# A retention recurrence with a feed-forward block: the first two batches worked by halves of the heads, with the first weights in between

## Chip, cores, metric

One core of one Trainium2 chip. The metric is device microseconds of one execution, median over runs, each listed with its mean granted TensorE clock. Times of single runs stand in one column, the span of the profile (first to last instruction) is 1.7 to 2.2 us shorter than the time. The later calls ran on chips 1, 11 and 12; the record does not name the chip of the first call. Kernels of one call ran on the same chip beside runs of the kernel before.

## The reference, cut to what matters

```python
B, H, S, D = 4, 8, 768, 64
for t in range(S):                                   # per batch and head
    state = gamma * state + outer(k[t], v[t])
    y[t] = (q[t] @ state) / sqrt(D)
x = y.transpose(0, 2, 1, 3).reshape(B * S, H * D)    # 3072 x 512
h = x @ w_in                                         # 512 x 2048
out = maximum(0.01 * h, h) @ w_out                   # 2048 x 512
```

The weights come in as 64-bit floats (as words) and are turned into 32-bit ones on the chip; the recurrence is worked in chunks of 128 tokens: scores, a mask, values, and a state handed from chunk to chunk.

## The kernel before: the parts that the change touches

The kernel starts with four batches of chunk 0, and with the first four pieces of the weights, which all have to be loaded. `score` is 16 small matmuls (64x64 tiles), `values` 8, a step of `direct` is 4 matmuls of 128x128 by 256 columns with weights (each fp32 matmul shows as two instructions in a trace). `keep_busy(n)` issues n matmuls on zeros into a bank that nobody reads: filler.

```python
load_qk(0, 0); load_v(0, 0); load_qk(0, 1); load_v(0, 1)   # 0.52 + 0.26 MB each
load_piece(0); load_piece(1)                                # weights, 0.52 MB each
load_qk(0, 2); load_v(0, 2); load_piece(2); load_piece(3, words)
...
keep_busy(7)
score(0, 0)
# tables and spread: the decays, three matmuls on 8 rows of the table
masked(0, 0)
...
score(0, 1); values(0, 0); masked(0, 1); decay_v(0, 1)
keep_busy(1)
next_powers()                       # ScalarE: exponents of a piece
taken(0, 0, x)                      # VectorE: tokens into x
values(0, 1)
next_mantissas(lambda: taken(0, 1, x))   # VectorE: mantissas of the piece
next_powers()
score(0, 2)
keep_busy(3)
steps = direct(0, 0, x, parts[0][1], 0)
next(steps)                         # first product with weights
next_mantissas()
...
next(steps); values(0, 2); ...; score(0, 3); ...
next(steps)
for b in range(B): first_state(b, sums0)      # sums for the states
values(0, 3)
run(steps, {})                                # last product step
taken(0, 3, x); first_states_taken(sums0); add_sums(0, last=False)
```

## Time and profile before

| | before |
|---|---|
| time, median of 6 runs of the first call | 666.90 us (666.56 to 667.01) |
| span of the profile | 664.9 us |
| TensorE in the chain that ended last | 99% |
| first real matmul, first product with weights | 4.63 us, 14.09 us |
| sums for the states end, reads of chunk 1, batch 1 begin | 23.54 us, 33.45 us |

The lines that carry this are in the prediction.

### The profile page before, as it was taken

To read this page: it belongs to the slowest core of one execution; us is meant where nothing else is said; L and a number is where in the kernel's file an instruction comes from. 1 tells how busy PE (TensorE), PEld (TensorE's weight loads), DVE (VectorE), ACT (ScalarE), POOL (GpSimd) and SP (SyncE) were. 2 spreads that over 40 slices of the span, in tenths; PEclk is the share of its full clock that TensorE was granted. 3 is DMA by queue.
4 is the path that set the end of the run, shared out by engine and by line. 5 is a ranking of instruction groups with operands and counts; after the bars stand their busy time and mean duration, and the time that the engine had idled before them with its cause. 6 is when DMAs were issued, how large, how long until landed. Compare 5 with 4: busy or idle time off the path is not lost.

```text
span 664.9 us, 10405 instructions
## 1 busy us (share of the span) xinstructions
PE 659.4 (99%) x4505; PEld 573.6 (86%) x4505; DVE 373.9 (56%) x570; ACT 175.8 (26%) x322; POOL 20.1 (3%) x22
## 2 busy tenths in 40 slices
PE   8999999999999999999999999999999999999998
PEld 5888888888888888888888888888888888888886
DVE  5789969889888676325543613663431444431342
ACT  5854555264261002212201311210221220221210
POOL 0000000000000111001000100100100000000000
PEclk9999999999999999999999999999999999999999
DMA  8920312313222453003012100301300001000001
GB/s 327 403 97 33 126 64 79 112 65 113 109 85 75 166 184 127 1 1 128 1 46 81 64 1 1 127 1 64 128 1 0 2 0 45 19 1 1 0 1 63
DMA packets 15758, 48.92 MB, mean 74 GB/s; under 512 B 1753, under 2 KB 2009, under 8 KB 15713
## 3 DMA queue, kind: packets, MB, share of 16 engines
q1 hardware_dynamic: 15696, 48.24, 20.1%
q8 instruction: 35, 0.57, 0.3%
q14 instruction: 11, 0.08, 0.0%
q10 hardware_dynamic: 16, 0.02, 0.0%
HBM read 41.97 MB, written 6.29 MB: 73 GB/s over the span
## 4 chain that ended last, share of the span: by engine, by line
PE 99%; DMA 1%; DVE 0%; issue 0%
PE B_o L414 13%; PE A_o L414 13%; PE C_o L414 12%; PE C_h L414 12%; PE B_h L414 12%; PE A_h L414 12%; PE D_o L414 6%; PE D_h L414 6%; PE ap L165 4%; PE yp L193 4%; PE d L436 2%; PE yp L184 2%; PE yp L208 1%; DMA qk<-in_qk_dram 1%; PE sums L208 0%; PE idle L626 0%
## 5 line engine op out<-in xcount | busy, mean ns | idle before, releaser
L414 PE MATMUL A_h<-x,w 128*128 128x256 f32 x368 | 87.0, 379 | 0.0
L414 PEld LDWEIGHTS A_h<-x,w 128*128 128x128 f32 x368 | 69.9, 190 | 9.6 <-issue 0.2
L414 PE MATMUL A_o<-g,w 128*128 128x256 f32 x288 | 68.0, 379 | 0.0
L449 ACT ACTIVATE g<-g 128x512 f32<-128x512 f32 x69 | 42.0, 630 | 92.4 <-DVE g L361 92.4
L414 PEld LDWEIGHTS A_o<-g,w 128*128 128x128 f32 x288 | 54.8, 190 | 7.4
L454 ACT COPY m<-A_h 128x512 f32<-128x512 f32 x23 | 13.4, 582 | 143.6 <-PE A_h L414 103.9
L361 DVE TENSOR_TENSOR m<-m,B_h 128x512 f32<-128x512 f32 x23 | 15.8, 686 | 55.5 <-PE B_h L414 55.5
L361 DVE TENSOR_TENSOR m<-m,B_o 128x512 f32<-128x512 f32 x16 | 11.0, 685 | 63.9 <-PE B_o L414 63.9
L238 DVE TENSOR_TENSOR x<-yp,dec 128x512 f32<-128x512 f32 x24 | 16.4, 689 | 49.7 <-PE yp L208 35.6
L414 PE MATMUL C_h<-t,w 128*128 128x256 f32 x184 | 44.1, 383 | 0.0
L414 PE MATMUL B_h<-x,w 128*128 128x256 f32 x184 | 44.1, 383 | 0.0
L414 PE MATMUL B_h<-t,w 128*128 128x256 f32 x184 | 43.5, 379 | 0.0
L414 PE MATMUL D_h<-t,w 128*128 128x256 f32 x184 | 43.5, 379 | 0.0
L414 PE MATMUL C_h<-x,w 128*128 128x256 f32 x184 | 43.5, 379 | 0.0
L414 PEld LDWEIGHTS C_h<-t,w 128*128 128x128 f32 x184 | 34.5, 190 | 5.5 <-issue 0.9
L414 PEld LDWEIGHTS B_h<-t,w 128*128 128x128 f32 x184 | 35.0, 190 | 4.7
L414 PEld LDWEIGHTS D_h<-t,w 128*128 128x128 f32 x184 | 35.0, 190 | 4.7
L414 PEld LDWEIGHTS C_h<-x,w 128*128 128x128 f32 x184 | 35.0, 190 | 4.7
L414 PEld LDWEIGHTS B_h<-x,w 128*128 128x128 f32 x184 | 34.5, 190 | 5.0 <-issue 0.3
L364 DVE TENSOR_TENSOR gd<-g,gd 128x512 f32<-128x512 f32 x48 | 37.1, 773 | 1.7
L170 DVE TENSOR_TENSOR am<-ap,mask 128x1024 f32<-128x1024 f32 x24 | 28.5, 1220 | 10.8 <-PE ap L165 10.8
L414 PE MATMUL B_o<-gd,w 128*128 128x256 f32 x144 | 34.0, 379 | 0.0
(118 smaller groups left out, 1019.0 us busy)
## 6 DMA issues: line engine op xcount, KB each, us to landing
raw<-in_weights_dram SPq DMA_DIRECT2D x31, 512.0 KB, 4.3
qk<-in_qk_dram SPq DMA_DIRECT2D x19, 512.0 KB, 3.8
kv<-in_kv_dram SPq DMA_DIRECT2D x17, 512.0 KB, 4.4
out_dram<-o SPq DMA_DIRECT2D x23, 256.0 KB, 2.1
in<-in_qk_dram SPq DMA_DIRECT2D x3, 512.0 KB, 8.7
in<-in_kv_dram SPq DMA_DIRECT2D x3, 512.0 KB, 8.5
kv<-in_kv_dram SPq DMA_DIRECT2D x4, 256.0 KB, 7.0
o_in<-in_qk_dram SPq DMA_DIRECT2D x2, 512.0 KB, 8.6
```

Of the source, the lines that this page charges most:

```text
L165: nc.tensor.matmul(ps[ts(u, 64), j, a, :], lhsT=x[ts(j, 64), 1, a, ts(u, 64)], rhs=x[ts(j, 64), 0, a, :])
L170: nc.vector.tensor_tensor(out=am.rearrange("p j a t -> p (j a) t"), in0=scores[c, b].rearrange("p j a t -> p (j a) t"), in1=mask.unsqueeze ...
L184: nc.tensor.matmul(ps[ts(i, 64), j, m, :], lhsT=st[b][ts(j, 64), a, :], rhs=x[ts(j, 64), 0, a, :], start=(m == 0), stop=False, skip_group_ ...
L193: nc.tensor.matmul(ps[ts(i, 64), j, m, :], lhsT=y[:, 1, 2 * a + j, :], rhs=am[:, j, a, :], start=(c == 0 and m == 0), stop=True, skip_grou ...
L208: nc.tensor.matmul(sp[ts(j, 64), a, :], lhsT=y[:, 0, 2 * a + j, :], rhs=y[:, 1, 2 * a + j, :], start=start, stop=True, skip_group_check=True)
L238: nc.vector.tensor_tensor(out=blocks, in0=ps[:, :, 0 : HP // 2, :], in1=gq, op=ALU.mult)
L361: nc.vector.tensor_tensor(out=out, in0=a, in1=b, op=ALU.add)
L364: nc.vector.tensor_tensor(out=out, in0=a, in1=b, op=ALU.subtract)
L414: nc.tensor.matmul(half, lhsT=block(w, sa)[:, k, ts(i, 128)], rhs=rhs[:, k, :], start=(first and (i == 0 or split) and n == 0 and k == 0), ...
L436: nc.tensor.matmul(banks[r][:, i, :], lhsT=block(2 * u, r + 2 * kh)[:, k, ts(i, 128)], rhs=x[:, 2 * kh + th, k, :], start=(step == 0 and i ...
L449: nc.scalar.activation(g[:, i], g[:, i], AF.Prelu, alpha=0.01)
L454: nc.scalar.copy(out=got["m1"], in_=ps)
```

## The change

Intent: let TensorE begin products with weights sooner. Only half of the first two batches is loaded ahead of the first two pieces of the weights; that half is scored, masked and multiplied, then comes the first product step, then the second half, and so on. For that, q, k and v of four heads lie next to each other in one array of 8 KB rows. All filler but the one at the start goes. The diff, cut to its core:

```diff
-    rows = t[0:H, 1:3].rearrange(...)[:, 0 : decay.shape[1]]
-    nc.scalar.dma_start(out=rows, in_=decay)
-    load_qk(0, 0)
-    load_v(0, 0)
-    load_qk(0, 1)
-    load_v(0, 1)
+    rows = t[:, 1:3].rearrange(...)[:, 0 : decay.shape[1]]
+    nc.gpsimd.memset(rows, 0.0)
+    nc.scalar.dma_start(out=rows[0:H], in_=decay)
+    nothing = t[:, 0, 0, 0:64].bitcast(BF16)
+    nc.vector.memset(t[:, 0, 0, 0:64], 0.0)
+    load_half(0, 0, 0)            # 3 KB of every 8 KB row: 0.39 MB
+    load_half(0, 1, 0)
     load_piece(0)
     load_piece(1)
+    load_half(0, 0, 1)
+    load_half(0, 1, 1)
 ...
-    keep_busy(7)
-    score(0, 0)
+    keep_busy(8)
+    score(0, 0, 0)                # first half of the heads
     # tables
+    score(0, 1, 0)
     # spread
+    first_values(0, (0,)); first_values(1, (0,))
+    begin_mantissas()
+    first_tokens_taken(0, x, (0,)); first_tokens_taken(1, x, (0,))
+    end_mantissas()
+    score(0, 0, 1)                # second half
     steps = direct(0, 0, x, parts[0][1], 0)
     next(steps)                   # k, kh swapped: the first half is enough for it
+    ...; score(0, 1, 1); next(steps); ...
+    first_values(0, (1,)); first_values(1, (1,)); ...; score(0, 2); next(steps); ...
 ...
     score(0, 3)
-    next(steps)
+    run(steps, {})                # last product step
+    first_values(3)
     sums0 = two_banks("sums0")
     for b in range(B):
         first_state(b, sums0)
-    values(0, 3)
-    run(steps, {})
```

## The prediction

> **What bounds the kernel now.** I read the page first, then the chain that ended last (whole span, then the first 45 us), then the order of instructions in time for the first 45 us, then the transfers.
>
> ```profile
> span 664.9 us, 10405 instructions
> PE 659.4 (99%) x4505; PEld 573.6 (86%) x4505; DVE 373.9 (56%) x570; ACT 175.8 (26%) x322; POOL 20.1 (3%) x22
> PE 99%; DMA 1%; DVE 0%; issue 0%
> ```
>
> TensorE is the bound: the chain is TensorE from its first real matmul to the end, and after 45 us it waits for nobody by more than 0.3 us. So only the start can pay, and a microsecond won there reaches the end only if nothing takes it back. The chain of the start, by start and length, says where the dead time is:
>
> ```profile
> 0.80 3.78 DMA qk<-in_qk_dram
> 4.63 1.75 PE ap L165 x32
> 7.88 1.03 PE ap L165 x32
> 8.91 1.02 PE yp L193 x16
> 9.94 0.32 PE idle L626
> 11.48 0.70 DVE x L238
> 12.23 1.10 PE ap L165 x32
> 13.34 0.75 PE idle L626 x3
> 14.09 3.45 PE d L436 x16
> 19.60 1.92 PE d L436 x8
> 21.53 2.02 PE sums L208 x64
> 23.54 0.88 PE yp L193 x16
> 24.42 3.65 PE d L436 x16
> ```
>
> The reader is to see that from 4.63 to 14.09 us TensorE does filler twice (0.32 and 0.75; these matmuls write a bank nobody reads) and stands for VectorE once (0.70); with small gaps that is about 2.0 us that serve nothing. From 14.09 on the chain has no gap. All that the change can win is a part of these 2.0 us.
>
> The filler is there because of the transfers:
>
> ```profile
> 9.55 0.69 ACT L334 ACTIVATE w<-raw 128x512 f32<-128x512 uint16 x1 [1.05 <-DMA raw<-in_weights_dram]
> 4.00:4.50 0.50, 0.50 (x2) 0.00 (x0) 0.00 (x0) 0.00 (x0) 0.00 (x0) 1.00 0.40 115
> 7.00:7.50 0.50, 0.50 (x2) 0.05 (x1) 0.50 (x1) 0.00 (x0) 0.00 (x0) 1.00 1.10 430
> ```
>
> ScalarE begins to unpack the first piece of the weights when it lands, at 9.55. In the table of stretches (last column GB/s) the transfers run at 410 to 430 once going, but between 4 and 6 us only at 115 to 300. From issue plus time to landing of each single load I get landing against the bytes queued up to it: 0.52 MB at 4.6 us, 0.79 at 5.5, 1.31 at 7.6, 1.57 at 8.3, 2.10 at 9.6, 2.62 at 10.9, 3.15 at 12.1, 3.93 at 14.0, 4.46 at 15.4, 5.24 at 17.3.
>
> **What the Trainium skill says.** "TensorE: Matmul & The Clock Gate", Part 1 (the HAM clock gate), says that the array runs at half rate until it has been busy for about 4 us. The trace agrees: the first score's matmuls take 417 to 471 ns until 5.9 us, then 269, which is why it takes 1.75 us against 1.03 later. The same page, section "HAM oscillation", says an idle stretch of some 3.4 us brings the half rate back; no run here shows that yet, and it matters, as the change takes all filler but the first out. "DMA: Bandwidth & Descriptors", the anatomy of one DMA, gives about 2 us fixed plus bytes at 436 GB/s, fitted on the GpSimd path. Here the first 512 KB took 3.78 us, against 3.2 by that fit, and the steady rate was 410 to 430; I use the landings of this trace.
>
> **The change, part by part.**
>
> Transfers. Before: qk0, v0, qk1, v1 (1.57 MB) stood ahead of the first piece of weights. After: two half-batches of 0.39 MB each (q, k and v of four heads) stand ahead. By the landings above: first half-batch near 4.1, second 5.5, weights piece 0 (1.31 MB) 7.6 instead of 9.55, piece 1 (1.84 MB) 8.9, the second halves (2.23 and 2.62 MB) 9.9 and 10.9, piece 2 12.1, piece 3 13.4, batches 2 and 3 at 15.4 and 17.3, as before. The bytes are the same.
>
> Warm-up. The zeroed tile is 64 columns instead of 256 and comes first on VectorE, so the filler begins near 1.1 instead of 1.40; eight at 0.427 end near 4.5. Score work begins at 4.5 instead of 4.63.
>
> TensorE to the first product with weights. Half score, cold: 0.85, to 5.4. Tables 0.31 + 0.22, to 5.9. Half score of batch 1: two scores in a row took 1.91 and one 1.03, so a half is 1.03 - 0.44 = 0.59, to 6.5. Spread 0.96, to 7.45. The two half values lie side by side, 1.02, to 8.5. Then the next half score waits for its data, 9.9 (1.4 dead), and ends at 10.5. The first product needs piece 0: landed 7.6, ScalarE 0.69, a copy 0.59 put between, 0.63 + 0.63, with hops 10.25, then VectorE 0.69: 10.95 (0.45 dead). VectorE's own work before that (two masks of 0.69, a decay near 0.4, 0.42 + 0.69 of the piece, two half takes of 0.42) fits in between.
>
> TensorE from there. One product step by itself is 1.92 (the row at 19.60), while two in a row are 3.45: now each step stands alone between small matmuls. 10.95 + 1.92 (step 0) + 0.59 + 1.92 (step 1; piece 1 ready at 12.9, in time) + 1.02 (both half values) + 1.03 (score 2), then a wait of 0.15 for piece 2, + 1.92 + 1.0 + 1.03 + 1.92 + 0.95 + 2.02 (the sums for the state) = 26.4; the first step of the second token half ends at 28.35. Before, that step ended at 28.07. So the same work is done 0.3 us later: 1.0 us of filler and the 0.7 of waiting are gone, but 1.4 + 0.45 + 0.15 of new waits and some 0.7 of smaller groups (0.47 for split product steps, 0.12 for each split score) take their place.
>
> After that. TensorE's order is the same, but VectorE's start of the next chunk moved: the sums used to end at 23.54, ahead of the last values, now they come last, at 26.4. Behind them stand on VectorE the states 1.22, the weight sums 2.14, then 4.23 from the mask of chunk 1, batch 0, to the end of the mask of batch 1 (in the trace 29.17 to 33.40): 26.45 + 1.25 + 2.1 + 4.23 = 34.05. The matmuls that read the state of batch 1 reuse the bank which that mask frees, and began at 33.52, 0.12 after it. They now begin near 34.15, 0.65 later. From 45 us on I expect no change: the loads of the later chunks become one of 1 MB instead of two of 512 KB, but GpSimd is idle for some 50 us between them. The hand sum is +0.65, or 667.5.
>
> **The rivals.**
>
> First rival: the weights come sooner than my landings say. The slow stretch of the transfers from 4 to 6 us may belong to what is issued then and not to the time. Piece 0 is the third transfer instead of the fifth; at 0.41 MB per us from the second half's 5.5 it lands at 6.8. The first product then starts at 10.2 to 10.5 (score of the second half at 9.2 to 9.9) and everything after is 0.5 to 0.7 earlier: 666.9, or less if the half groups cost less than 0.59. For it: the steady 430 GB/s directly after. Against it: the same number of transfers is issued by the same queue in the same first 3 us.
>
> Second rival: the change does what it was made for, the dead time falls from 2.0 to under 1.0, and nothing is handed back later: 665.5 to 666. It needs the landings of the first rival, cheap switching between tile sizes, and the sums to end before 25.6. Against it: the product cannot start earlier than about 3.3 us after piece 0 has landed (ScalarE's four steps and VectorE's one), whatever TensorE does.
>
> Third rival: without filler inside, TensorE's clock falls to half for a while. The dead stretches that I find are 1.4 and 0.45 us, under the 3.4 us of the skill; a fall would cost about 2 us and give 669. I hold it for unlikely.
>
> **Range and chances.** The hand sum gives +0.65; the first rival, about as likely, gives 0; the second gives -1. I set the point at 666.9, so no change within what I can tell, and the range 665.5 to 668.1, which holds all but the clock rival. Two per cent is 13 us, and all the dead time there is makes 2: 0.99 within 2%, 0.005 on either side.
>
> **What would show it right or wrong.** Piece 0's first step on ScalarE near 7.6 (rival one: 6.8); the first product near 10.95 (10.3) instead of 14.09; TensorE idle before the second half score, released by its load; the first step of the second token half ending near 28.35; the reads of chunk 1, batch 1, released by VectorE's mask near 34.15, with a TensorE wait of some 0.3 us that was not there; no filler after 4.5 us and no matmul slowed to 417 ns after 6 us. A wait that I did not find, before 45 us, or one in the later chunks where the 1 MB loads land, would make it wrong; so would a first product that comes later than 11.5.

## More of the kernel before

The order of instructions in time: the columns are start, length, engine, line, operation, tiles, shapes, count, and in brackets the idle time of that engine before it and what ended it. First the table of decays, which waits for nothing, then the reads of the state of chunk 1, batch 1 (as weight loads, PEld), which just wait for VectorE's mask:

```profile
6.31 0.38 PE L638 MATMUL tables<-t 8*128 8x8 f32 x2
...
33.45 0.43 PEld L184 LDWEIGHTS yp<-in,states 64*64 64x64 f32 x16 [0.17 <-DVE am L170]
```

## The result, and the profile after

| | before | after |
|---|---|---|
| median of 6 runs, us | 666.90 | 669.41 |
| all runs, us | 666.56 to 667.01 | 668.09, 668.24, 669.33, 669.50, 669.94, 670.38 |
| clock of these runs | (profiled run: 1.000) | 1.000, 1.000, 0.997, 0.997, 1.000, 0.995 |
| span of the profiled run (666.64 and 668.24 us) | 664.9 | 666.2 |

The ratio is 1.0036, with an interval of 1.0023 to 1.0049. Such ratios are the mean time of one kernel's runs over that of the other's of the same rounds, so not quite the ratio of the medians. The change made the kernel slower by 2.5 us in the median: "within 2%" held, the range (665.5 to 668.1) did not.

Two things are mixed in these 2.5 us. The two runs with the lowest times are 1.2 to 1.3 us above the kernel before; the other four lie 1.1 to 2.3 us above those two. I take the first part from the profile, which fell on a low run.

The page of the kernel after, its first lines and the chain's shares:

```profile
span 666.2 us, 10350 instructions
PE 659.4 (99%) x4502; PEld 572.4 (86%) x4502; DVE 372.1 (56%) x573; ACT 175.6 (26%) x323; POOL 22.2 (3%) x25
PE 97%; DVE 1%; DMA 1%; ACT 1%; issue 0%; POOL 0%; POOLq 0%
```

TensorE is as long at work as before (659.4), but now 3% of the chain is other engines. TensorE in order of time:

```profile
5.21 0.79 PE L182 MATMUL ap<-in 64*64 64x128 f32 x16 [0.57 <-DMA in<-in_heads_dram]
7.10 0.36 PE L703 MATMUL tables<-t 128*128 128x8 f32 x2 [1.09 <-DMA t<-decay_dram]
...
8.21 1.13 PE L711 MATMUL spread<-t 128*128 128x512 f32 x2
...
11.93 1.99 PE L494 MATMUL d<-x,w 128*128 128x256 f32 x8 [0.76 <-DVE w L415]
```

The first product with weights does come sooner, at 11.93 instead of 14.09. But the first half score starts later than the full one did (5.21 against 4.63), and TensorE waits 1.09 us for the table of decays, which nobody waited for before. The chain names that load, and what follows the sums:

```profile
1.58 5.39 DMA t<-decay_dram
...
25.59 1.89 PE sums L254 x64
...
27.50 1.23 DVE states L269
...
33.69 1.23 DVE am L191
...
34.96 0.67 PE yp L208 x16
```

The sums now end at 27.5 instead of 23.54, VectorE's states wait for them, and the reads of chunk 1, batch 1, begin at 34.96, 1.5 us later than before. From there the two kernels run nearly in step; the spans differ by 1.3, so some 0.2 comes back later.

### The profile page after: what moved, and what is told of

Same layout as the page of the kernel before. It is cut to its first block, busy times and chain, and to the rows that moved or that the text cites. A ratio compares the mean times of both kernels' runs of the same rounds, so it can differ in the third digit from the quotient of the medians.

```text
span 666.2 us, 10350 instructions
## 1 busy us (share of the span) xinstructions
PE 659.4 (99%) x4502; PEld 572.4 (86%) x4502; DVE 372.1 (56%) x573; ACT 175.6 (26%) x323; POOL 22.2 (3%) x25
## 4 chain that ended last, share of the span: by engine, by line
PE 97%; DVE 1%; DMA 1%; ACT 1%; issue 0%; POOL 0%; POOLq 0%
PE B_o L472 12%; PE A_o L472 12%; PE C_o L472 12%; PE C_h L472 12%; PE B_h L472 12%; PE A_h L472 12%; PE D_o L472 6%; PE D_h L472 6%; PE ap L182 3%; PE yp L215 3%; PE d L494 2%; PE yp L208 2%; PE yp L254 1%; DMA t<-decay_dram 1%; PE yp L226 0%; PE sums L254 0%
## 5 line engine op out<-in xcount | busy, mean ns | idle before, releaser
L283 DVE TENSOR_TENSOR x<-yp,dec 128x512 f32<-128x512 f32 x20 | 13.7, 688 | 47.4 <-PE yp L254 35.2
L422 DVE TENSOR_TENSOR gd<-g,gd 128x512 f32<-128x512 f32 x48 | 35.4, 737 | 1.7
L158 POOL TENSOR_TENSOR in<-in,dec 128x512 f32<-128x512 f32 (+1 forms) x19 | 20.9, 1102 | 459.3 <-DMA in<-in_heads_dram 260.5
```

The source lines that it names most:

```text
L158: engine.tensor_tensor(out=v[:, a:z], in0=v[:, a:z], in1=g[:, a:z].unsqueeze(3).to_broadcast([128, z - a, H // 2, D]), op=ALU.mult)
L283: nc.vector.tensor_tensor(out=blocks, in0=ps[:, :, 0 : HP // 2, :], in1=gq, op=ALU.mult)
L422: nc.vector.tensor_tensor(out=out, in0=a, in1=b, op=ALU.subtract)
```

## The experiments

All kernels gave correct results. I call a run disturbed when it is over 1.0 us above the fastest run of its own kernel (the kernel before and the changed kernel: of all their runs), and clean otherwise. The line is a rough one: two runs of e4 with a clock of 0.997 fall below it, and two of e6 lie just on it. "Cold" means at half rate: the matmuls take about twice as long as the same ones later. The counts are gathered here, and used below.

| run | what it is | runs | fastest, us | median, us | disturbed |
|---|---|---|---|---|---|
| before, all calls | 7 filler matmuls at the start | 40 | 666.42 | 666.90 (first call); 666.92; 667.84; 666.91 (chips 1, 11, 12) | 11 |
| changed, both calls | 8 at the start | 11 | 668.09 | 669.41; 670.18 | 8 |
| e1_decay | changed, decays early | 6 | 667.49 | 668.69 | 3 |
| e2_filler | changed, filler in the later waits | 6 | 668.10 | 669.55 | 3 |
| e3_sums | changed, sums ahead | 6 | 667.53 | 669.45 | 5 |
| e4_two | e1 and e3 | 6 | 666.71 | 668.16 | 3 |
| e5_full | e2 with 10 at the start | 6 | 668.09 | 668.26 | 0 |
| e6_best | e4 with 10 and later filler | 6 | 667.28 | 667.79 | 1 |
| e7_contig | changed, halves in one piece | 4 | 667.63 | 668.45 | 2 |
| e8_bare | before, no later filler | 6 | 666.53 | 666.73 | 2 |
| e10_warm | before, 10 at the start | 5 | 667.00 | 667.16 | 0 |
| e11_all | e6 with e7 | 5 | 667.65 | 667.86 | 0 |
| e12_lean | e4 with e7, 8 at the start | 6 | 666.97 | 669.10 | 5 |
| e13_nine | before, 9 at the start | 6 | 666.49 | 666.91 | 0 |
| e14_ten | changed, 10 at the start | 6 | 667.97 | 668.18 | 1 |
| e15_four | before, 4 at the start | 6 | 669.34 | 669.72 | 6 (counted from the fastest run of the kernel before, 2.9 us or more over it) |

The kernel before had 0 of 6 disturbed runs in the first call, and 2 of 11, 7 of 12 and 2 of 11 on chips 1, 11 and 12. (On chip 11, two calls share most of these runs.)

### The theory and its rivals

T: the load of the decays comes late and holds the tables, and with them the first product. H: the sums at the end of the chunk hand a loss back through VectorE. C: the spread of the runs is the array clock. Against T stands that ScalarE's chain behind the first weights sets the first product anyway; against H, that VectorE's wait only falls into a loss that TensorE has already; against C, that the transfers scatter.

### e1_decay

```diff
-    rows = t[:, 1:3].rearrange(...)[:, 0 : decay.shape[1]]
-    nc.gpsimd.memset(rows, 0.0)
-    nc.scalar.dma_start(out=rows[0:H], in_=decay)
+    rows = t[0:H, 1:3].rearrange(...)[:, 0 : decay.shape[1]]
+    nc.scalar.dma_start(out=rows, in_=decay)
```

> The changed kernel with the decay table on 8 rows again and its load issued at once, as before (no zero fill of 128 rows on GpSimd ahead of it). Theory T (the small load of the decays, issued at 1.58 us behind four big ones, lands at 6.96 and holds the tables, the decayed values and the first product): the load lands near 3 to 5 us, the tables run right after the first half score (near 6.0 instead of 7.10), the first product with weights moves from 11.93 to about 11.0, and the profiled run gets 0.6 to 1.0 us shorter than the changed kernel's best (668.1), so 667.1 to 667.5. Rival R1 (ScalarE's chain after the first piece of weights sets the first product anyway): the tables come early, but the first product stays at 11.7 to 11.9 and the time at 668. Theory C (the spread of the runs, 668.1 to 670.4, is the array clock that comes to full rate late or falls back, because TensorE waits between 4.6 and 12 us): here one wait of 1.1 us goes away, so fewer runs lie over 1 us above the fastest.

TensorE in order of time, run e1:

```profile
6.17 0.38 PE L702 MATMUL tables<-t 8*128 8x8 f32 x2
...
11.08 1.99 PE L494 MATMUL d<-x,w 128*128 128x256 f32 x8 [0.48 <-DVE w L415]
```

The wait ahead of the tables is gone, the first product comes 0.85 sooner, and the fastest run is 0.60 under the changed kernel's. T holds. The rival R1 does not: in both profiles ScalarE's copy of the spread, which hangs on the tables, starts 0.02 us after the spread ends (at 9.37, in e1 at 8.46), when its first step on the weights is already done, and the first product follows from there.

How a load of 24 KB can take 5.4 us is seen in the packets of its queue, counted by half microsecond: issued at 0.80 (kernel before and e1), its 16 packets move between 1.5 and 2.5 us; issued at 1.58, after the zero fill, none moves before 5.0, and the last after 6.5. In those 0.8 us the first two half-batches have been issued.

In e1 the first piece of weights also landed sooner (ScalarE began on it at 7.55 instead of 8.12). That is no accident of one run: with the halves read from wide rows, ScalarE began at 7.29 to 7.61 in the three profiles with the early issue (e1, e4, e6) and at 7.92 to 8.65 in the six with the late one; why, no run shows. It bears on the gain: at 8.12 + 0.68 the copy could not have begun before 8.80, so some 0.35 of the 0.85 us needed the sooner weights too.

On the spread of the times nothing can be concluded: three of six runs were disturbed, against four of six of the changed kernel's first call.

### e2_filler

```diff
     score(0, 0, 0)
+    keep_busy(2)
     # tables
-    score(0, 0, 1)
+    score(0, 0, 1)        # after 2 filler matmuls into its own bank
-    steps = direct(0, 0, x, parts[0][1], 0)
+    steps = direct(...)   # after 1 filler matmul into its own bank
```

> The changed kernel with filler matmuls put into its three waits (2 ahead of the tables, 2 ahead of the second half score, 1 ahead of the first product), nothing else. Theory C: the runs come together: all at 668.0 to 668.6 with a clock of 1.000, where the changed kernel has 668.1 to 670.4 with three clocks of 0.995 to 0.997. Rival (the spread comes from the transfers or the waits themselves, not from the clock): the spread stays near 2 us, median 669.4. The fastest run should not be faster than the changed kernel's fastest by more than 0.2 under either, since the filler takes away no wait.

Half right. No run had a clock under 1.000 any more (the changed kernel had four of eleven, so six runs do not prove it), but the runs fell into two groups: 668.10, 668.13, 668.39 and 670.70, 670.84, 670.92. So there are two kinds of disturbance: one that shows as a lower mean clock, and one of 2.5 us that the clock's record does not show.

### e3_sums and e4_two

```diff
     score(0, 3)
     ...
-    run(steps, {})
-    first_values(3)
     sums0 = two_banks("sums0")
     for b in range(B):
         first_state(b, sums0)
     load(1, 3)
+    first_values(3)
     decay_v(1, 0, nc.scalar)
+    run(steps, {})
```

> The changed kernel with the sums for the states ahead of the last values, and the last product step behind both, as before the change; the start is left alone. Theory H (part of the loss is handed back after the start: the sums come last, VectorE begins the states and the weight sums later and holds the reads of chunk 1, batch 1, until 34.96): the fastest run gets 0.5 to 1.0 us shorter (667.1 to 667.6), the reads of batch 1 no longer wait for VectorE's mask or by less than 0.2, the spread of the runs stays. Rival R2 (TensorE's own work has moved by the whole 1.3 us and VectorE's wait only falls into it): the time stays at 668.1 for the fastest.

> Both mends together: decay load first on 8 rows, and the sums ahead of the last values. If T and H are both right and add up: fastest run 1.3 to 1.9 us under the changed kernel's, 666.2 to 666.8, so level with or just under the kernel before (666.9). If they are one and the same slack: no better than the better of the two single ones. Theory C expects the spread of single runs to remain where TensorE still waits for loads between 8 and 11 us.

The fastest run of e3 is 0.56 under the changed kernel's, that of e4 1.38 under it (the sum of the two alone is 1.16). So H holds too, and the two add up. The profiles of both fell on disturbed runs, so the clean times are the evidence (e3 has only one clean run); the clean profile of e6 below, which has both mends, shows that the wait for VectorE is back to 0.17. Part of the gain of e3 is on TensorE: the last product step and the next one are neighbours again, 3.65 us for both instead of two of 1.92. With both mends the kernel is level with the kernel before (666.71 against 666.42 for the fastest run on that chip), not under it.

The profile of e4 fell on a run with clock 0.997, and shows what that is. The table of stretches; columns are the stretch, its length, busy time of TensorE, weight loads, VectorE, ScalarE and GpSimd with counts, granted TensorE clock, share and rate of the transfers:

```profile
7.00:8.00 1.00, 1.00 (x4) 0.24 (x4) 1.00 (x3) 0.39 (x1) 0.53 (x1) 1.00 1.01 414
...
8.50:9.00 0.50, 0.50 (x8) 0.50 (x6) 0.31 (x1) 0.50 (x2) 0.00 (x0) 0.50 1.10 442
9.00:10.00 1.00, 0.86 (x9) 0.48 (x7) 0.53 (x2) 0.97 (x3) 0.06 (x1) 0.50 1.02 411
...
12.00:13.00 1.00, 1.00 (x7) 0.81 (x5) 0.90 (x2) 0.81 (x2) 0.00 (x0) 1.00 1.06 432
```

The granted clock falls to 0.50 soon after 8.0 us and is back before 12. And yet TensorE was busy from 5.2 to 8 without a hole; before that it had one of 0.56 us, at 4.64.

The profile of e3 was cold in the other way: the spread took 2.07 us and the values after it 1.98 instead of 1.13 and 1.09, until about 13 us, with the clock recorded as 1.000. So half rate from the very start goes unrecorded, and the mean clock names only runs in which the clock falls after it had been full.

### e5_full, e6_best, e7_contig, e8_bare

e5 is e2 with `keep_busy(10)` at the start. e6 has the edits of e1 and e3, `keep_busy(10)`, and the later filler of e2 without the two ahead of the tables.

> The changed kernel with 10 filler matmuls at the start instead of 8 (to 5.3 us, so that the wait of 0.57 us ahead of the first half score is filled too) and the filler in the three later waits. The run with filler in the later waits alone had no clock under 1.000 any more, but still two groups of runs: three at 668.1 to 668.4 and three at 670.7 to 670.9. Theory C1 (the second group are runs in which the array did not come to full rate at 5 to 6 us, because the first filler ends before the first real work and leaves a hole): all six runs at 668.1 to 668.7. Rival (the late warm-up comes from where the clock's window happens to lie at the start, hole or no hole): still one to three of six runs near 670.8.

> All mends together: decays on 8 rows and loaded at once, sums ahead of the last values, 10 filler matmuls at the start, 2 ahead of the second half score and 1 ahead of the first product. If T, H and C1 are right: all six runs at 666.5 to 667.0, so level with the kernel before (666.9) with a spread under 0.6 us; the change then has no gain left to give even when every loss that I found is mended. If the late warm-up is luck alone: 666.6 for the fast ones and 669 for one to three of six.

On a chip where the kernel before had 7 of 11 disturbed runs in the same call, e5 had none of 6 (668.09 to 668.55), as expected under C1. The reason that C1 gives is not shown: in e5's profile the first half score is still cold, to about 6.5 us, with no hole ahead of it. In e6 three runs were at 667.3, two at 668.3 and one at 668.75 with clock 0.997, so none lay 2 us or more above the others, but the fastest was 667.28, not 666.5 to 667.0: ten filler matmuls end at 5.4 us and hold the first half score back. Its profile, a clean one:

```profile
5.43 0.67 PE L184 MATMUL ap<-in 64*64 64x128 f32 x16
...
10.87 1.99 PE L498 MATMUL d<-x,w 128*128 128x256 f32 x8
...
33.51 0.42 PEld L210 LDWEIGHTS yp<-in,states 64*64 64x64 f32 x16 [0.17 <-DVE am L193]
```

The first product is 3.2 us sooner than before the change and the reads of batch 1 are where they were (33.51 against 33.45). So where do the 3.2 us go? The chains of the two profiles answer it. Most of it was never a gain: a half score (0.60), two groups of half values (1.02) and a score (1.03) that used to stand ahead of the first product now stand behind it, 2.65 us of work that is moved and not saved. The rest goes to product steps that stand alone (0.46 for the first two, 0.07 for the third) and to a wait of 0.10. Together that is 3.28 us, and the sums begin at 21.59 instead of 21.53.

```diff
 # e7: an array of its own for the first two batches
-        fetch(c, b, m * HALF, (m + 1) * HALF)
+        nc.sync.dma_start(out=heads[c, b][:, m * HALF : (m + 1) * HALF], in_=first_in[m, b])
```

> The changed kernel with the first two batches' halves read from an own array in which each half-batch of 393 KB lies in one piece, instead of 3 KB of every 8 KB row; nothing else. In the changed kernel the first half-batch lands 4.4 us after its issue (at 5.2), though 0.52 MB of q and k before landed after 3.8, and the transfers ran at 150 to 220 GB/s from 2.5 to 4.5 us where they ran at 330 to 385 before. Theory L (it is the layout: pieces of wide rows are read slower while the transfers start): the first half-batch lands after 3.3 to 3.8 us, the rate between 2.5 and 4 us is over 300, and the first product starts up to 0.6 earlier. Rival (it is the start of the queue, whatever is read): landing again near 4.4 and the same rates.

The stretch from 2.5 to 4 us, in the kernel before, the changed kernel and e7 (the last column is GB/s):

```profile
2.50:4.00 1.50, 1.50 (x5) 0.45 (x3) 0.00 (x0) 0.19 (x1) 0.00 (x0) 1.00 0.91 362
```

```profile
2.50:4.00 1.50, 1.50 (x5) 0.46 (x3) 0.00 (x0) 1.00 (x1) 0.00 (x0) 1.00 0.88 164
```

```profile
2.50:4.00 1.50, 1.50 (x5) 0.45 (x3) 0.00 (x0) 1.00 (x1) 0.00 (x0) 1.00 1.04 342
```

The engines are as busy, but they move 164 GB/s where the source is a 3 KB piece of an 8 KB row, and 342 where it is in one piece. The first half score starts at 4.58 instead of 5.21. (The profile fell on a disturbed run, so its first product, at 12.93, says nothing.) Theory L holds for the start (later, past 6 us, the wide rows run at 416 as well). The fastest run is 0.46 under the changed kernel's.

```diff
 # e8, from the kernel before
-    keep_busy(1)
     next_powers()
 ...
     score(0, 2)
-    keep_busy(3)
```

> The kernel before with its four later filler matmuls taken out (1 after the first values, 3 ahead of the first product); the seven at the start stay. Question: is the fall of the clock in the changed kernel due to the filler that it took out? If yes: here too several of six runs show a clock of 0.995 to 0.997 and lie 0.8 to 2.5 us over the fastest, which is at 665.8 to 666.6 (up to 1.1 us of filler gone from the chain, though part of it only covered waiting for a load). Rival (what matters are the holes between 4.6 and 7.1 us, which this kernel hasn't): all runs within 0.7 us and clock 0.999 to 1.000.

Two of six disturbed (one at clock 0.994), about as in the kernel before (7 of 11 in this call); the fastest, 666.53, is 0.3 under its. So, as far as six runs tell, taking the later filler out is not what disturbs the runs. The profile fell on a run with the clock never raised at the start. The order of instructions, then two stretches:

```profile
7.34 2.05 PE L644 MATMUL spread<-t 8*128 8x512 f32 x2
...
11.23 3.04 PE L193 MATMUL yp<-am,kv 128*64 128x128 f32 x26
```

```profile
6.00:8.00 2.00, 2.00 (x17) 1.48 (x10) 1.30 (x2) 0.00 (x0) 0.00 (x0) 1.00 0.96 350
...
12.00:14.00 2.00, 2.00 (x22) 2.00 (x20) 1.27 (x3) 1.94 (x5) 0.00 (x0) 1.00 1.02 411
```

TensorE is busy without a hole from 1.40 us on, and the spread at 7.34 and the values at 11.23 still run at half rate. Holes cannot be the reason here. What TensorE does between 4.6 and 14 us are matmuls on 64x64 tiles, on 8 rows or into 64 columns; only the filler and the products with weights fill the array. That this is why it stays cold is a guess: no run here changed the tiles alone.

### e9_after, e10_warm, e11_all, e12_lean

e9 is the changed kernel unchanged. e10 is the kernel before with the change's small zeroed tile and `keep_busy(10)`. e11 is e6 with the edit of e7. e12 has the edits of e1, e3 and e7 and `keep_busy(8)`.

> The changed kernel as it is, beside the kernel before on this chip. On the last chip the kernel before itself had 7 of 11 runs at 667.8 to 670.2, on the first none of 6; so part of the difference on record may be luck of the clock. Theory A: the clean runs (clock full from 6 us on) of the two differ by 1.2 to 1.4 us (668.1 against 666.8), and disturbed runs (over 0.6 us above the cleanest of their kernel) are about as frequent in both on one chip, so that the median's 2.5 us is 1.3 of the kernel and the rest of the clock. Theory B: the change itself makes disturbed runs more frequent: at least four of six here against at most a third of the kernel before's runs of the same call.

Of five runs four were disturbed (669.69 to 670.57), against 2 of 11 of the kernel before beside them; the clean one is 668.19. Theory B holds: the changed kernel is disturbed more often. Its profile shows the spread at half rate (the clean profile has 1.13 and 1.09):

```profile
9.05 2.08 PE L711 MATMUL spread<-t 128*128 128x512 f32 x2
11.06 1.68 PE L226 MATMUL yp<-am,in 128*64 128x128 f32 x16
```

> The kernel before with ten filler matmuls at the start instead of seven, begun at 1.05 us like the changed kernel's (64 zeroed columns), else as it was. With ten at the start none of 12 runs of two kernels on the last chip stayed cold until 13 us, while the kernel before did in 3 of 11. Theory W (the late warm-up depends on how long the dense filler at the start lasts, since the small matmuls after it do not bring the clock up: in one profile TensorE was busy from 1.4 us without a hole and still cold at 13): no run of six above 669, clean runs 667.0 to 667.6, because the filler now ends at 5.4 instead of 4.5 and part of the 0.8 us is taken up by the later filler's place. Rival (chance of the chip): as many runs above 669.5 as the kernel before has in this call.

All five at 667.00 to 667.46, as expected, though the kernel before had only two disturbed runs in this call, both with a lower clock.

> All mends (decays early on 8 rows, sums ahead of the last values, ten filler matmuls at the start, three later) and the first halves read from an array of their own in one piece. In the run with that array alone the first half-batch landed by 4.6 instead of 5.2 and the first piece of weights 0.4 earlier. If the first product hangs on the first piece of weights (landing near 7.2, then 3.3 us): first product at 10.4 to 10.6 instead of 10.87, clean runs 666.7 to 667.0, none above 668.5. Rival: the transfers of the first 7 us move the same bytes, so the weights land at 7.5 as before and nothing is won: 667.3.

> Decays early on 8 rows, sums ahead of the last values, first halves in one piece; filler as in the changed kernel (eight at the start, none later). Clean runs: without the array of its own 666.7; with it the start is 0.3 to 0.5 earlier if the loads land earlier, so 666.2 to 666.5, under the kernel before's clean runs (666.4 to 667.1). Disturbed runs by the clock: two or three of six, up to 3 us above, as with eight filler matmuls before.

Both missed in their times: e11's fastest is 667.65 and e12's only clean run 666.97. In e11 the first product came at 11.62 instead of 10.4 to 10.6, in e12 the first piece of weights landed at 8.20 and the second half at 10.6. From e12, ScalarE's first step on the weights (from the chain: start, length, what), then the second half score (from the order of instructions):

```profile
8.22 0.67 ACT m_x L395
```

```profile
10.62 0.67 PE L183 MATMUL ap<-in 64*64 64x128 f32 x16 [2.02 <-DMA in<-in_first_dram]
```

What is gained at the start of the transfers is lost between 4 and 6 us (206 GB/s in e12 against 286 in e1). Why, I have not found out. In e12 the chain of the start is the load of the weights. In e11 no load stands in it: the first half score and the tables are still cold (1.06 and 0.80 us in the chain, against 0.60 and 0.53 in e6), which makes 0.73 of the 0.75 us that its first product comes after e6's. Faster tables alone would have won at most 0.26 of that, as ScalarE is done with its first step on the weights only at 8.76, 0.28 before it copies the spread.

As a pair, on one chip with the same loads, e11 with ten filler matmuls and three later ones had no disturbed run of five, e12 with eight and a hole of 2.0 us had five of six, all with a lower clock. The two differ in both things, so the pair does not part them.

### e14_ten, e15_four, e13_nine

```diff
 # e14, from the changed kernel          # e15, from the kernel before      # e13, from e10
-    keep_busy(8)                        -    keep_busy(7)                  -    keep_busy(10)
+    keep_busy(10)                       +    keep_busy(4)                  +    keep_busy(9)
```

> The changed kernel with ten filler matmuls at the start instead of eight, no later filler, nothing else. If the length of the dense start decides the late warm-up and the holes decide the fall-back: no run cold until 13 us (none above 670 with clock 1.000), but still some with clock 0.995 to 0.997 between 668.8 and 669.7; clean runs 668.1 to 668.4. If the length does both: all runs at 668.1 to 668.6. If the holes do both: as many above 670 as before.

> The kernel before with four filler matmuls at the start instead of seven (they end at 3.3, then a hole of 1.3 us to the first score), nothing else. If the length decides: most of six runs at 669.5 to 670.5 with clock 1.000, cold until about 13 us, where the kernel before has at most a third. If the length does not matter: as the kernel before in this call.

> The kernel before with nine filler matmuls at the start begun at 1.05 us (they end at about 5.0). Ten gave five runs at 667.0 to 667.5, all clean, against 666.7 to 667.0 of the kernel before's clean runs, as they held the first score back by 0.8 us. Nine should hold it back by 0.4: clean runs 666.8 to 667.1, none above 667.6. If it is so, it is the version to keep: level with the clean runs of the kernel before and without its disturbed ones (mean under the kernel before's mean on a chip where that has any).

e14: five runs at 667.97 to 668.50 and one at 669.38 with clock 0.997; none above 670 with the clock recorded as 1.000. e15: all six at 669.34 to 670.44. TensorE in order of time, e15 and then e13:

```profile
1.39 1.89 PE L626 MATMUL idle<-t 128*128 128x512 bf16 x4 [1.39 <-DVE t L621]
...
7.47 2.05 PE L644 MATMUL spread<-t 8*128 8x512 f32 x2
```

```profile
1.05 4.02 PE L626 MATMUL idle<-t 128*128 128x512 bf16 x9 [1.05 <-DVE t L594]
...
6.75 1.10 PE L644 MATMUL spread<-t 8*128 8x512 f32 x2
```

In the kernel before, four, seven, and nine or ten filler matmuls at the start gave 6 of 6, 11 of 40 and 0 of 11 disturbed runs. Runs of the late kind (about 3 to 4 us over, with the clock recorded as 1.000) are 6, 4 and 0 of these. In the changed kernel eight gave 8 of 11, half of them with the clock recorded as 1.000, and ten 1 of 6, with a lower clock. Pooled over all kernels, 20 of 91 runs with seven or eight filler matmuls lie over 1.0 us above the fastest of their kernel with the clock recorded as 1.000, and none of 34 with nine or ten. So a longer dense start and fewer late warm-ups go together. That the length alone does it is not shown: in e15 a hole of 1.40 us opens ahead of the first score, in e14 one of 0.57 closes, and e13 and e10 also begin 0.35 us sooner; by themselves, their 0 late runs of 11 against 4 of 40 could be chance.

Nor does the length set the moment at which the full rate comes. From e14, its ten filler matmuls, and from e11 the first half score (that of e6, above, took 0.67):

```profile
1.05 4.04 PE L683 MATMUL idle<-t 128*128 128x512 bf16 x10 [1.05 <-DVE t L653]
```

```profile
5.43 1.13 PE L185 MATMUL ap<-in 64*64 64x128 f32 x16
```

Ten filler matmuls that are cold throughout take 4.45 us (e5, e6, e10, e11). In e14 the last of them are already fast, so the full rate came between 4 and 5.1 us; in e6 it came at about 5.4, in e5 at about 6.5, in e11 at about 6.9. So ten filler matmuls do not end the cold time sooner; in these runs they only kept it from lasting until 13 us.

e13 costs nothing in the clean runs (666.49 to 667.18, against 666.62 to 667.01 of the kernel before on that chip) and has no disturbed one; its ratio to the kernel before, which had 7 of 12 disturbed there, is 0.9983 (0.9967 to 1.0000). By these six runs it is the version to keep, and it has nothing of the change in it but the filler's earlier start.

## Why the prediction was wrong, step by step

- **What bounds the kernel, and that only the 2 us of dead time before 14.09 could be won: right.** TensorE's busy time is 659.4 in both; all differences arise before 36 us but for some 0.2. "Within 2%" followed from the 2 us alone, as 2% is 13 us.
- **"Half score, cold: 0.85, to 5.4. Tables 0.31 + 0.22, to 5.9": failed.** I gave the tables no wait for their load. I had read the zero fill in the diff, but took the load of decays to be small and hence quick. It lands at 6.96; the tables end at 7.68, 1.8 later than I had them. e1 gives 0.85 of it back at the first product, and 0.60 in the time.
- **"First half-batch near 4.1": failed.** It lands at 5.2. I took landing to depend on bytes alone; the layout of the source more than halves the rate at the start (164 GB/s, and 342 in e7, where nothing else is changed). The first rival, that the weights come sooner than the byte count says, went the other way: 8.1 against my 7.6 (7.55 with the decays early, in e1).
- **First product "10.95" against 11.93, step of the second token half "28.35" against 29.38**: the late decays and the late loads together; the rest of that sum was right (17.40 us between the two as I had it, 17.45 as it came). The sentence that lists what is gone and what is new does not close as it stands (2.7 less 1.7 is 1.0, not 0.3): it leaves out the earlier start and the shorter cold score. The sum before it is the one to go by.
- **The loss behind the sums: right in kind.** I had the reads of chunk 1, batch 1, 0.65 later than before; they came 1.5 later, as everything ahead of them was later by 1.0. e3 and e4 show that mending it is worth 0.56 to 0.78.
- **Clean total**: hand sum +0.65; measured +1.2 to +1.3. I had weakened the hand sum to 666.9 by half believing in sooner weights; that was the wrong direction.
- **The third rival, the clock, "I hold it for unlikely": failed, and it is why the range was missed so far.** Without it the result would have been about 668.2, just past the range's edge. I looked for holes of 3.4 us and found none. What went wrong needs no such hole: runs warm up late, even with TensorE busy throughout (e8), with four, seven or eight filler matmuls at the start and not with nine or ten; and the clock falls back after a stretch of small matmuls with one hole of 0.56 us (e4) or after one of 2.0 (e12). Of the 2.5 us of the median some 1.3 are the kernel and 1.2 the disturbed runs. The kernel before has them too, 11 of 40, but none of its first six; so its quiet first runs hid them.

Left open: why the changed kernel with eight filler matmuls (3.6 us) is disturbed more often than the kernel before with seven (3.2). The holes that follow at 4.65 and 6.0 us are the obvious difference, but e1, which lacks the second, still had three of six, and e14, which has the second and ten filler matmuls, had one; the share of each is not settled. Also open is why the transfers of e11 and e12 lost their sooner start again between 4 and 6 us.

## What to carry to other kernels

When a start is bound by loads, splitting the first piece of work in two moves the first heavy matmul forward (here by 3.2 us in e6), but the work that it overtakes still has to be done, and product steps that stand alone cost more (1.92 each against 3.45 for two). The smallest load on the path, issued late behind big ones, cost 0.60 us here, where the split won nothing: issue small tables first. Keep the work that the next stage's critical engine needs (here the sums for the states) ahead of work that nobody waits for. Judge such a kernel by all its runs and not by one quiet median; here the recorded clock alone did not tell, as a run that was cold from the start to 13 us has 1.000. Where the start is light, try longer dense filler: of the 34 runs with nine or ten matmuls none was late by its time.

## What the Trainium skill lacked or had wrong

- "TensorE: Matmul & The Clock Gate", Part 1: the full rate comes after some 3.4 us of sustained matmuls. Here TensorE was busy from 1.40 us without a hole and was still at half rate at 11 to 14 us in e8. The matmuls after the filler used small tiles; whether these count as busy the page does not say, and no run here changed them alone.
- The same page, section "HAM oscillation": no gap over about 3.4 us. To keep to that was not enough here: in e4 the granted clock fell to 0.50 soon after 8.0 us and was back before 12, though the longest hole since the filler began was 0.56 us.
- The same Part 1 has the transition at around 4 us of sustained matmuls, give or take 0.5 from run to run. Here, with ten filler matmuls from 1.05 us, it came between 3 and 4.1 us after that in e14 and nearly 6 after it in e11, where small matmuls follow the filler; in e8 it came only at about 14. With four filler matmuls (1.9 us) all six runs were late; with nine and ten (4.0 to 4.5 us) none of 34 lay 1.5 us or more above the fastest of its kernel.
- "DMA: Bandwidth & Descriptors", Queues, rings and completion order: the engines go round the queues by packets. Here a load of 24 KB from its own queue, issued at 1.58 us behind the first big loads, moved no packet before 5.0 us and landed after 5.39; issued at 0.80 it had moved by 2.5. Why the turns did not reach it sooner, no run shows.
- No page has that a source of 3 KB pieces of 8 KB rows starts at 164 GB/s (2.5 to 4 us) against 342 for the same bytes in one piece (e7), and runs at 416 later.
